# A linear-attention and rational-FFN kernel: the second batch's k'v products in one visit, its o's one slot each, casts of x by converting transfers

## The chip, the cores and the metric

The kernel runs on one core of one Trainium2 chip. A core has five engines that run their own instruction lists side by side and wait for each other by semaphores: TensorE (PE, matmuls), VectorE (DVE), ScalarE (ACT), GpSimd (POOL) and SyncE (SP, which here only issues transfers). The metric is the device time of one execution in microseconds (us); lower is better. Before the change it is 879.95 us, the median of 3 runs (879.93 to 879.99).

## The reference

Eight batches of 576 tokens, 8 heads of 64. Each head's attention is linear: k'v is one 64x64 matrix per head, o is q times it, and o is normalised per token and head. The 4608 tokens of 512 features then pass a feed-forward layer of 2048 hidden units whose activation is a rational function.

```python
kv  = einsum('bhsd,bhse->bhde', k, v)
out = einsum('bhsd,bhde->bhse', q, kv)
rms = sqrt(mean(out * out, axis=-1) + 1e-06)
x   = (out / rms * g_norm)          # heads side by side: [4608, 512]
h   = x @ w_in                      # [4608, 2048]
P   = a[0] + a[1]*h + a[2]*h**2 + a[3]*h**3
Q   = 1.0 + abs(b[0])*abs(h) + abs(b[1])*h**2
y   = (P / (Q + 1e-06)) @ w_out     # [4608, 512]
```

The two weights come as 64-bit words and are turned into fp32 on the chip.

## The kernel before

**Tiles and slots.** The tokens are cut into 9 tiles of 512: tile t (0 to 7) holds the first 512 tokens of batch t, and tile 8 the 64 tokens that each batch has left over. Each tile passes 16 slots, one for each chunk c of 128 hidden units. In slot (t, c) ACT and DVE turn h(t, c) into g(t, c) (`ew_a` to `ew_d`), PE makes the h of the next slot (`gemm1`, names h, lines L527 to L533), and adds the g of two slots before into the output's accumulators (`gemm2`, names acc, lines L590 to L601, LAG = 2). Beside this, the attention of the *next* tile is made, a step here and a step there, by the tables `attention` (tiles 1 and later) and `attention0` (tile 0). What each engine does is a list in program order: from `tc.manual_schedule()` on nothing is moved.

**Tile 0** is special. The weights are loaded, turned to fp32 (ACT: `signed` L206, `lowbits` L213; DVE: `conv_b1` L224, `conv_add` L228) and later split into a high and a low part while it runs; a table `schedule` says in which slot. Until the split is there the matmuls are plain fp32: a 128x512 matmul then stands as two records of 0.43 us in the trace. The split of x for tile 0 (`split_x0`) makes a high part by an ACT cast (L258), and a low part from it by a POOL negation (L250) and an accumulating transfer on POOL's queue (L251). It is first used by h(0, 8).

**The attention of tile 1, made during tile 0.** The four head pairs p go one after the other. `att_kv1` makes k'v of one pair (names kvp, 20 small matmuls, L351) in slots 1, 3, 5 and 7, and ACT copies it to kvf (L270). `att_o` makes o of that pair (names op, L430) in slots 2, 4, 6 and 8, and ACT squares and copies it (L438, L439). kvp and op share one PSUM buffer (`ps_at`, tag "at", one buffer), so each waits until ACT has read the one before. The transposed q of a pair, qr, has one buffer too: `fetch_q` for pair p + 1 is issued on SP right behind o of pair p (`fetch_next_q`), and waits for it. Means (ms, L451) and reciprocal roots stand in slot 9, the products of the leftover tokens (rest, L379) in slot 10. Tiles 2 and later make all four pairs of k'v in one visit (`att_kv4`).

**The front.** Before slot 0, batch 0's own attention is made in two halves of 256 tokens. Sums over a head (`first_ms`, L692) and the spreading of the reciprocal roots to all rows (`first_rb`, L708) work in NBLK blocks of BW tokens.

**SP's queue.** All loads go through SP, in program order: an entry that waits for a buffer holds up all behind it. A transfer also waits until the eighth one before it has landed.

Of the kernel before, what the change touches and what calls it, by code (L numbers as in the profile page):

```python
# [7 lines left out]
F32 = mybir.dt.float32  # L8
# [15 lines left out]
def linear_attention_then_rational_ffn(  # L24
# [38 lines left out]
    NC = 7  # L63
    HW = TW // 2
    MAIN = 8 * P
    NBLK = 4
    BW = HW // NBLK
    kv0 = [wpool.tile([P, 2, MAIN], F32, tag=g, name=f"first_{g}") for g in ("g4", "g5")]
    qa0 = wpool.tile([P, NPAIR * HW + NC], F32, tag="g6", name="first_qa")
# [100 lines left out]
        made[schedule["wi", c][1] + 1].append(("wi", c, None))  # L170

    EARLY = 8
    ON_VECTOR = (("wi", 6),)

    def unsplit(t, c):
        return t == 0
# [77 lines left out]
    def split_x0(g):  # L254
        pool, tag = ((xpool, "xA"), (wpool, "e"))[g]
        xt = pool.tile([P, 2, 2, TW], F32R, tag=tag, name=f"x_0_{g}")
        of = x0[:, 2 * g:2 * g + 2]
        ACT.copy(xt[:, :, 0], of)  # L258
        x.setdefault(0, []).extend((xt[:, p, 0], xt[:, p, 1]) for p in range(2))
        lows.append((xt[:, :, 1], xt[:, :, 0], of))  # L260

# [2 lines left out]
    def split_kv(t, pairs, ps):  # L266
        n = pairs.stop - pairs.start
        made = [ps[js, 0:n * D].rearrange("p (n d) -> p n d", n=n) for js in heads]
        for js, m in zip(heads, made):
            ACT.copy(kvf[js, pairs, js], m)  # L270
        if t == 1:
            return None
        for js, m in zip(heads, made):
            ACT.copy(kvh[js, pairs, js], m)

        def rest():
            for js in heads:
                DVE.tensor_tensor(kvl[js, pairs, js], kvf[js, pairs, js], f32(kvh[js, pairs, js]), ALU.subtract)
        return rest
# [28 lines left out]
    kvms, qrs, qs, sqs, rs, rbs, xf = {}, {}, {}, {}, {}, {}, {}  # L308

    def fetch_kv(t, p):  # L310
        tag, bufs = ("rb", 2) if p >= 2 and t > 1 else (f"kvm{p % 2}", 1)
        kvms[t, p] = work.tile([P, 2, 4, P], F32, tag=tag, name=f"kvm_{t}_{p}", bufs=bufs)
        nc.sync.dma_start(kvms[t, p], kv[t, p])

    def fetch_ends(t):
        kvms[t] = work.tile([P, 2, 3, P], F32, tag="kvt", name=f"kvt_{t}", bufs=1)
        nc.sync.dma_start(kvms[t], kv_rest[t])

    def fetch_q(t, p):
        qrs[t, p] = work.tile([P, TW], F32, tag="qr", name=f"qr_{t}_{p}", bufs=1)  # L320
        nc.sync.dma_start(qrs[t, p], qT[p, :, t * TW:(t + 1) * TW])

    def fetch_first_kv(t):
        if t < NB:
            for p in range(2):
                fetch_kv(t, p)
            fetch_ends(t)

    def fetch_last_kv(t, _):
        if t + 1 < NB:  # L330
            for p in range(2, NPAIR):
                fetch_kv(t + 1, p)
# [12 lines left out]
    def kv_products(t, ps, k, p):  # L345
        m = kvms.pop((t, p))
        ends = kvms[t][:, p // 2]
        for c in range(5):
            for js in heads:
                a, b = (m[:, 0, c], m[:, 1, c]) if c < 4 else (ends[:, 0], ends[:, 1 + p % 2])  # L350
                PE.matmul(ps[js, k * D:(k + 1) * D], a[:, js], b[:, js], start=(c == 0), stop=(c == 4))  # L351

    def att_kv1(t, p):
        ps = ps_at.tile([P, TW], F32, tag="at", name=f"kvp_{t}_{p}", bufs=1)
        kv_products(t, ps, 0, p)
        qs[t, p] = qrs.pop((t, p))
        split_kv(t, slice(p, p + 1), ps)

    def att_kv4(t, ps):
        if t >= NB:  # L360
            return None
        for p in range(NPAIR):
            kv_products(t, ps, p, p)
        fetch_first_kv(t + 1)
        return lambda: split_kv(t, slice(0, NPAIR), ps)

    def att_kv_of_third(t, _):
        return att_kv4(t, ps_at.tile([P, TW], F32, tag="at", name=f"kvp_{t}", bufs=1))() if t == 2 else None

    x_rest = dram.tile([NPAIR, P, NB * R], F32, tag="x_rest", name="x_rest", bufs=1)  # L370

# [50 lines left out]
    def att_o(t, p):  # L422
        if t == LAST:
            sqs[t, p] = work.tile([P, TW], F32, tag="at", name=f"sq_{t}_{p}", bufs=4)
            ACT.activation(sqs[t, p], xf[t, p], AF.Square)
            return
        ps = ps_at.tile([P, TW], F32, tag="at", name=f"op_{t}_{p}", bufs=1)
        q = qs.pop((t, p))
        if t == 1:
            PE.matmul(ps, kvf[:, p], q, start=True, stop=True)  # L430
        else:
            qh, ql = q
            PE.matmul(ps, kvh[:, p], ql, start=True, stop=False)  # L433
            PE.matmul(ps, kvl[:, p], qh, start=False, stop=False)  # L434
            PE.matmul(ps, kvh[:, p], qh, start=False, stop=True)  # L435
        sq = work.tile([P, TW], F32, tag="at", name=f"sq_{t}_{p}", bufs=4)
        xf[t, p] = xpool.tile([P, TW], F32, tag=f"xf{p}", name=f"xf_{t}_{p}")
        ACT.activation(sq, ps, AF.Square)  # L438
        ACT.copy(xf[t, p], ps)  # L439
        sqs[t, p] = sq  # L440
        if t == 1:
            if p + 1 < NPAIR:
                fetch_kv(t, p + 1)
            else:
                fetch_first_kv(t + 1)
            fetch_next_q(t, p)

    def att_ms(t, _):
# [41 lines left out]
    attention = {s: [] for s in range(NF)}  # L490
    for p in range(NPAIR):
        if p == 0:
            attention[0].append((att_kv_of_third, 0))
        attention[2 * p].append((att_q, p))
        attention[2 * p + 1].append((att_o, p))
        attention[(11, 12, 13, 13)[p]].append((att_norm, p))
    attention[3].append((fetch_last_kv, 0))
    attention[8] += [(att_rest, 0), (att_ms, 0)]
    attention[9].append((att_rstd, 0))
    fillat = {att_norm: 1, att_kv_of_third: 1, att_rest: 1, att_q: 1, att_rstd: 2}  # L500
    attention[10] += [(att_rd, 0), (att_rb, 0), (att_rb, 1)]

    fillat0 = {}
    attention0 = {s: [] for s in range(NF)}
    for f, at in ((att_kv1, [1, 3, 5, 7]), (att_o, [2, 4, 6, 8]), (att_ms, [9]), (att_rstd, [9]), (att_rd, [10]), (att_rest_first, [10]), (fetch_last_kv, [11]), (att_rb, [11, 11]), (att_norm, [12, 12, 13, 13])):
        for p, k in enumerate(at):
            attention0[k].append((f, p))

# [224 lines left out]
            DVE.tensor_copy(x0[:, p, halves[0]], o0[p][0])  # L733
    for u in at_slot(0, -1)[:1]:
        fetch_w(u)
    fetch_kv(1, 0)
    fetch_ends(1)
    fetch_q(1, 0)
    for u in at_slot(0, -1)[1:]:
        fetch_w(u)  # L740
    ms0 = ps_at.tile([P, TW], F32, tag="ms", name="ms_0", bufs=1)
    first_ms(0)
    for p in range(NPAIR):
# [40 lines left out]
    for i, (t, c) in enumerate(slots[:-1]):  # L784
        q_made = ew_a(t, c, ph)
        for todo in lows:

            tc.add_manual_dep(low_by_transfer(*todo).ins, q_made.ins.name, beside, reason="negated beside h")
        lows.clear()
        if i:  # L790
            ew_d(*slots[i - 1])
        rest = {0: [], 1: [], 2: []}
        shifts = []
        convs = [lambda u=(k, n), j=j: conv_add(u, both if j is None else (one, two)[j]) for k, n, j in made.get(i, [])]

        ew_b(t, c, ph, convs[:1])
        if i == LAG:
            ph = gemm1(0, i + 1)
        if i >= LAG:
            gemm2(*slots[i - LAG])  # L800
            if slots[i - LAG][1] == NF - 1:
                evacuate(slots[i - LAG][0])
        for u in at_slot(2, i):
            split_w(u)
        if i in (1, 3):
            split_x0(i // 3)
        if i == 0:
            ph = h0[1]
        elif i in (1, 3):
            ph = gemm1(0, i + 1)  # L810
        if t + 1 < NTILE:
            for step, p in (attention0 if t == 0 else attention)[c]:
                todo_dve = step(t + 1, p)
                if todo_dve:
                    rest[fillat0.get(step, 2) if t == 0 else fillat[step]].append(todo_dve)
            for u in at_slot(0, i):
                fetch_w(u)
        for u in at_slot(1, i):
            signed(u)
            lowbits(u, both, "V" if u in ON_VECTOR else "S")  # L820
            shifts.append(u)
        rest[2] += convs[1:]
        if t == 0 and c == NF - 3:
            rest[2] += [split(1, p) for p in range(NPAIR // 2)]
        if t and c == NF - 2:
            ph = h_last
        elif 4 <= i < len(slots) - 2:
            ph = gemm1(*slots[i + 1])
            if 0 < t < NTILE - 1 and c == NF - 3:
                h_last = gemm1(t, NF - 1)  # L830
        if c == NF - 2 and t < NTILE - 1:
            xl = [split(t + 1, p) for p in range(NPAIR // 2 if t == 0 else 0, NPAIR)]
            if t == 0:
                rest[0] += xl
            for k in range(2 if t else 0):
                rest[k].append(xl[k])
                rest[2].append(xl[2 + k])
        if i == 0:
            rest[2].append(lambda: conv_add(u2, one))
        rest[2] += [lambda u=u: conv_b1(u, both) for u in shifts]  # L840
        ew_c(t, c, lambda k: [f() for f in rest[k]])
# [55 lines left out]
```

## Time and profile before

| | |
|---|---|
| median of the runs | 879.95 us |
| the profiled execution's own time | 879.79 us |
| its span, first to last instruction | 877.7 us |
| granted TensorE clock | 0.999 |
| PE busy | 870.7 us, 99% |
| DVE busy | 757.7 us, 86% |
| ACT busy | 687.5 us, 78% |
| POOL busy | 73.3 us, 8% |
| SP's transfers | 65.81 MB |
| POOL's transfers | 9.44 MB |

In the rows that follow, times are us from the start of the span. A row of the chain of waits is "start, duration, what": the chain is followed back from the last instruction, at each step to what released it. A row of the timeline is "start, duration, engine line operation, out<-in, count", with the idle time before it and its releaser in brackets; PEld is PE's loading of weights, which runs ahead of the matmul, and SPq is SP's queue. The ends of matmuls are modelled, so a busy PE is read from the chain and from PEld's gaps, not from its busy share.

### The profile page before, as it was taken

Reading aid. Unit: us, or ns where it says so; the run is one execution under the profiler, and the core shown is the slowest. Engines: PE = TensorE matmul, PEld = TensorE weight load, DVE = VectorE, ACT = ScalarE, POOL = GpSimd, SP = SyncE. Lnnn points to the kernel's source line nnn. Section 1 sums busy time; section 2 is a strip of 40 time slices with the busy share of each in tenths; the row PEclk is TensorE's granted clock in tenths of the full one; section 3 lists DMA queues with packets and bytes.
Section 4 is the critical chain, followed back from the end, with each engine's and each line's share of the span. In section 5 each row is a group of like instructions: output and inputs, shape, how many; then the busy total and the mean of one; then the engine's idle time right before and its main releaser. Section 6 shows DMA issues by size and latency. Waiting matters only on the chain.

```text
span 877.7 us, 11994 instructions
## 1 busy us (share of the span) xinstructions
PE 870.7 (99%) x4468; PEld 683.9 (78%) x4468; DVE 757.7 (86%) x1185; ACT 687.5 (78%) x1142; POOL 73.3 (8%) x63
## 2 busy tenths in 40 slices
PE   9999999999999999999999999999999999999997
PEld 7545657888888888878888888888878887888886
DVE  4988998979987998879887998799879987998887
ACT  5999889877876788777877787768867786787665
POOL 2131435413000000000000000000000000000000
PEclk9999999999999999999999999999999999999999
DMA  9987638554122203040303111020102020201001
GB/s 364 406 262 226 145 73 216 138 127 97 60 73 90 50 6 115 30 122 1 119 19 104 31 61 72 25 50 17 69 12 50 13 84 1 49 1 49 1 0 49
DMA packets 32650, 76.27 MB, mean 87 GB/s; under 512 B 6032, under 2 KB 7568, under 8 KB 32592
## 3 DMA queue, kind: packets, MB, share of 16 engines
q1 hardware_dynamic: 29600, 65.81, 22.0%
q0 software_dynamic: 2848, 9.44, 5.9%
q8 instruction: 35, 0.57, 0.3%
q10 hardware_dynamic: 144, 0.26, 0.1%
q14 instruction: 23, 0.19, 0.1%
HBM read 55.45 MB, written 10.62 MB: 75 GB/s over the span
## 4 chain that ended last, share of the span: by engine, by line
PE 91%; DVE 5%; ACT 2%; issue 1%; DMA 1%; SPq 0%; ACTq 0%
PE h L531 14%; PE h L532 13%; PE h L533 13%; PE acc L599 12%; PE acc L601 12%; PE acc L600 12%; PE acc L590 5%; PE h L527 2%; PE kvp L351 2%; PE ms L451 1%; DMA first_g<-in_first_dram 1%; PE op L435 1%; PE op L433 1%; PE op L434 1%; DVE u L545 1%
## 5 line engine op out<-in xcount | busy, mean ns | idle before, releaser
L541 ACT ACTIVATE d<-h 128x512 f32<-128x512 f32 x143 | 85.6, 599 | 139.4 <-PE h L533 138.3
L543 DVE SCALAR_TENSOR_TENSOR q<-d,b1abs,q 128x512 f32<-128x512 f32 x143 | 107.2, 749 | 83.7 <-ACT q L542 83.5
L531 PE MATMUL h<-x,wihl 128*128 128x512 f32 (+1 forms) x420 | 166.2, 396 | 0.0
L532 PE MATMUL h<-x,wihl 128*128 128x512 f32 (+1 forms) x420 | 162.7, 387 | 0.0
L533 PE MATMUL h<-x,wihl 128*128 128x512 f32 (+1 forms) x420 | 162.6, 387 | 0.0
L599 PE MATMUL acc<-woh,gl 128*128 128x512 f32 x316 | 123.1, 389 | 0.1
L600 PE MATMUL acc<-wol,gh 128*128 128x512 f32 x316 | 122.9, 389 | 0.0
L601 PE MATMUL acc<-woh,gh 128*128 128x512 f32 x316 | 122.9, 389 | 0.0
L554 ACT ACTIVATE d<-q,bias 128x512 f32<-128x512 f32 x143 | 105.6, 738 | 13.9 <-DVE q L543 12.5
L544 ACT ACTIVATE u<-h,na 128x512 f32<-128x512 f32 x143 | 112.5, 787 | 0.0
L555 ACT ACTIVATE d<-d,bias 128x512 f32<-128x512 f32 x143 | 103.6, 725 | 4.7
L561 DVE SCALAR_TENSOR_TENSOR u<-u,na,d 128x512 f32<-128x512 f32 x143 | 106.7, 746 | 0.0
L551 DVE SCALAR_TENSOR_TENSOR u<-u,na,h 128x512 f32<-128x512 f32 x143 | 106.1, 742 | 0.6
L559 DVE SCALAR_TENSOR_TENSOR q<-q,d 128x512 f32<-128x512 f32 x143 | 98.4, 688 | 0.2 <-ACT d L555 0.2
L545 DVE TENSOR_TENSOR u<-u,h 128x512 f32<-128x512 f32 x143 | 98.0, 685 | 0.0
L542 ACT ACTIVATE q<-h,abg 128x512 f32<-128x512 f32 x143 | 97.9, 685 | 0.0
L531 PEld LDWEIGHTS h<-x,wihl 128*128 128x128 f32 x420 | 78.9, 188 | 24.0 <-issue 6.2
L532 PEld LDWEIGHTS h<-x,wihl 128*128 128x128 f32 x420 | 78.9, 188 | 17.0 <-issue 1.2
L533 PEld LDWEIGHTS h<-x,wihl 128*128 128x128 f32 x420 | 78.9, 188 | 16.2
L578 DVE TENSOR_TENSOR gl<-u,gh 128x512 fp32r<-128x512 f32 x127 | 90.8, 715 | 0.0
L567 DVE SCALAR_TENSOR_TENSOR u<-q,u 128x512 f32<-128x512 f32 x127 | 87.5, 689 | 2.5
L577 ACT CAST gh<-u 128x512 fp32r<-128x512 f32 x127 | 80.3, 632 | 3.5 <-DVE u L567 3.4
(170 smaller groups left out, 1403.0 us busy)
## 6 DMA issues: line engine op xcount, KB each, us to landing
kvm<-in_kv_dram SPq DMA_DIRECT2D x28, 512.0 KB
raw_wo<-in_w_out_dram SPq DMA_DIRECT2D x8, 1024.0 KB
out_dram<-ob SPq DMA_DIRECT2D x16, 512.0 KB
qr<-in_qT_dram SPq DMA_DIRECT2D x28, 256.0 KB
rb<-rd SPq DMA_DIRECT2D x28, 256.0 KB
raw_wi<-in_w_in_dram SPq DMA_DIRECT2D x6, 1024.0 KB
wihl<-wiw POOLq DMA_DIRECT2D x6, 512.0 KB, 4.7
kvt<-in_kv_rest_dram SPq DMA_DIRECT2D x7, 384.0 KB
```

The source lines that it names most:

```text
L531: PE.matmul(ph, wh, xl, start=(kc == 0), stop=False)
L532: PE.matmul(ph, wl, xh, start=False, stop=False)
L533: PE.matmul(ph, wh, xh, start=False, stop=(kc == NPAIR - 1))
L543: q_made = DVE.scalar_tensor_tensor(q, d, b1abs, q, ALU.mult, ALU.add)
L544: ACT.activation(u, ph, AF.Identity, bias=na[:, 2:3], scale=na[:, 3:4])
L545: DVE.tensor_tensor(u, u, ph, ALU.mult)
L551: DVE.scalar_tensor_tensor(u, u, na[:, 1:2], ph, ALU.add, ALU.mult)
L554: ACT.activation(d, q, AF.Ln, bias=bias[:, 2:3], scale=QSC)
L561: DVE.scalar_tensor_tensor(u, u, na[:, 0:1], d, ALU.add, ALU.mult)
L599: PE.matmul(o, gl[:, ss], wh, start=(c == 0), stop=False)
L600: PE.matmul(o, gh[:, ss], wl, start=False, stop=False)
L601: PE.matmul(o, gh[:, ss], wh, start=False, stop=(c == NF - 1))
```

## The change

- `att_kv1` is gone. All four pairs' k'v of the second batch are made by `att_kv4` in slot 3 of tile 0, and copied by two ACT copies of 64x4x64 instead of eight of 64x64. The o's stand in slots 4, 5, 6 and 7, and the leftover products in slot 9, ahead of the means.
- The loads follow: all of batch 1's k and v (kvm, kvt) are fetched in the front, behind the weights that are fetched there; batch 2's first two pairs of k and v are fetched by `att_kv4`, so in slot 3; qr of pairs 1 to 3 is still fetched behind the o before it.
- NBLK goes from 4 to 2: blocks of 128 tokens.
- The two high parts of tile 0's x are made by converting transfers on POOL's queue, issued in slot 0; the low parts follow one slot after the other.
- The low bits of the fourth pair of weight chunks (wi6) move from DVE to ACT.

```diff
-    NBLK = 4
+    NBLK = 2
-    ON_VECTOR = (("wi", 6),)
+    ON_VECTOR = ()
 def split_x0(g):
-        ACT.copy(xt[:, :, 0], of)
+        POOL.dma_start(xt[:, :, 0], of)
-        lows.append((xt[:, :, 1], xt[:, :, 0], of))
+        return xt[:, :, 1], xt[:, :, 0], of
 def fetch_kv(t, p):
-        tag, bufs = ("rb", 2) if p >= 2 and t > 1 else (f"kvm{p % 2}", 1)
+        tag, bufs = ("rb", 2) if p >= 2 else (f"kvm{p % 2}", 1)
-    def att_kv1(t, p): ...
-    def att_kv_of_third(t, _):
-        return att_kv4(t, ps_at.tile(...))() if t == 2 else None
+    def att_kv(t, _):
+        if t <= 2:
+            return att_kv4(t, ps_at.tile(...))()
 def att_o(t, p):
-            if p + 1 < NPAIR:
-                fetch_kv(t, p + 1)
-            else:
-                fetch_first_kv(t + 1)
             fetch_next_q(t, p)
-    for f, at in ((att_kv1, [1, 3, 5, 7]), (att_o, [2, 4, 6, 8]), (att_ms, [9]), (att_rstd, [9]), (att_rd, [10]), (att_rest_first, [10]), ...
+    for f, at in ((att_kv, [3]), (att_o, [4, 5, 6, 7]), (att_rest_first, [9]), (att_ms, [9]), (att_rstd, [9]), (att_rd, [10]), ...
 (front)
-    fetch_kv(1, 0)
-    fetch_ends(1)
-    fetch_q(1, 0)
     for u in at_slot(0, -1)[1:]:
         fetch_w(u)
+    fetch_first_kv(1)
+    fetch_last_kv(0, 0)
+    fetch_q(1, 0)
 (slots)
-        if i in (1, 3):
-            split_x0(i // 3)
+        if i == 0:
+            x0_lows = [split_x0(g) for g in range(2)]
+        if i in (1, 2):
+            lows.append(x0_lows[i // 2])
```

PE around slots 3 to 5 of tile 0, before: kvp_1_1 is k'v of the second batch's pair 1, op_1_1 its o, kvm and kvt are k and v, acc with g_0_2 is the output's part of chunk 2.

```order
L527 MATMUL h_0_4_522<-x0_144,wiw4_405 128x512 x4
L351 MATMUL kvp_1_1_527<-kvm_1_1_487 64x64 x8
L351 MATMUL kvp_1_1_527<-kvt_1_238 64x64 x2
L590 MATMUL acc_0_0_473<-wow2_452,g_0_2_499 128x512
L590 MATMUL acc_0_1_474<-wow2_452,g_0_2_499 128x512
L590 MATMUL acc_0_2_475<-wow2_452,g_0_2_499 128x512
L590 MATMUL acc_0_3_476<-wow2_452,g_0_2_499 128x512
L430 MATMUL op_1_1_571<-qr_1_1_489,kvf_128 128x512
L527 MATMUL h_0_5_585<-x0_144,wiw4_405 128x512 x4
```

The same place on PE now:

```order
L518 MATMUL h_0_4_475<-x0_144,wiw4_383 128x512 x4
L351 MATMUL kvp_1_480<-kvm_1_0_242 64x64 x8
L351 MATMUL kvp_1_480<-kvt_1_246 64x64 x2
L351 MATMUL kvp_1_480<-kvm_1_1_244 64x64 x8
L351 MATMUL kvp_1_480<-kvt_1_246 64x64 x2
L351 MATMUL kvp_1_480<-kvm_1_2_248 64x64 x8
L351 MATMUL kvp_1_480<-kvt_1_246 64x64 x2
L351 MATMUL kvp_1_480<-kvm_1_3_250 64x64 x8
L351 MATMUL kvp_1_480<-kvt_1_246 64x64 x2
```

All four pairs stand in one run behind h(0, 4); acc with g_0_2 and op_1_0 follow, and op_1_1 stands one slot, h(0, 5) and acc with g_0_3, behind op_1_0.

SP's queue before, from the load of the chunk pair wo6 to the q of pair 2 of the second batch (qr_1_2; raw_ are weights):

```order
L191 DMA raw_wo6_439<-in_w_out_dram 128x2x512
L313 DMA kvm_1_1_487<-in_kv_dram 128x1024
L321 DMA qr_1_1_489<-in_qT_dram 128x512
L191 DMA raw_wi12_491<-in_w_in_dram 128x2x512
L191 DMA raw_wo8_493<-in_w_out_dram 128x2x512
L191 DMA raw_wi14_540<-in_w_in_dram 128x2x512
L313 DMA kvm_1_2_577<-in_kv_dram 128x1024
L321 DMA qr_1_2_579<-in_qT_dram 128x512
```

And now, from wo6 to wo10:

```order
L191 DMA raw_wo6_402<-in_w_out_dram 128x2x512
L191 DMA raw_wi12_444<-in_w_in_dram 128x2x512
L191 DMA raw_wo8_446<-in_w_out_dram 128x2x512
L313 DMA kvm_2_0_521<-in_kv_dram 128x1024
L313 DMA kvm_2_1_523<-in_kv_dram 128x1024
L317 DMA kvt_2_525<-in_kv_rest_dram 128x768
L191 DMA raw_wi14_529<-in_w_in_dram 128x2x512
L321 DMA qr_1_1_564<-in_qT_dram 128x512
L191 DMA raw_wo10_566<-in_w_out_dram 128x2x512
```

The q of pair 1 went from before wi12 to behind wi14, and three loads of the third batch's k and v stand ahead of it.

More of the change, by code (lines that the diff above doesn't have):

```diff
@@ L351, in kv_products @@
                 PE.matmul(ps[js, k * D:(k + 1) * D], a[:, js], b[:, js], start=(c == 0), stop=(c == 4))
[L353 to L357, printed above, removed]
     def att_kv4(t, ps):
@@ L365, in att_kv4 @@
         return lambda: split_kv(t, slice(0, NPAIR), ps)
-    def att_kv_of_third(t, _):
-        return att_kv4(t, ps_at.tile([P, TW], F32, tag="at", name=f"kvp_{t}", bufs=1))() if t == 2 else None
+    def att_kv(t, _):
+        if t <= 2:
+            return att_kv4(t, ps_at.tile([P, TW], F32, tag="at", name=f"kvp_{t}", bufs=1))()
     x_rest = dram.tile([NPAIR, P, NB * R], F32, tag="x_rest", name="x_rest", bufs=1)
@@ L427, in att_o @@
         ps = ps_at.tile([P, TW], F32, tag="at", name=f"op_{t}_{p}", bufs=1)
-        q = qs.pop((t, p))
+        q = qrs.pop((t, p)) if t == 1 else qs.pop((t, p))
         if t == 1:
@@ L492, in linear_attention_then_rational_ffn @@
         if p == 0:
-            attention[0].append((att_kv_of_third, 0))
+            attention[0].append((att_kv, 0))
         attention[2 * p].append((att_q, p))
@@ L499, in linear_attention_then_rational_ffn @@
     attention[9].append((att_rstd, 0))
-    fillat = {att_norm: 1, att_kv_of_third: 1, att_rest: 1, att_q: 1, att_rstd: 2}
+    fillat = {att_norm: 1, att_kv: 1, att_rest: 1, att_q: 1, att_rstd: 2}
     attention[10] += [(att_rd, 0), (att_rb, 0), (att_rb, 1)]
@@ L504, in linear_attention_then_rational_ffn @@
     attention0 = {s: [] for s in range(NF)}
-    for f, at in ((att_kv1, [1, 3, 5, 7]), (att_o, [2, 4, 6, 8]), (att_ms, [9]), (att_rstd, [9]), (att_rd, [10]), (att_rest_first, [10]), (fetch_last_kv, [11]), (att_rb, [11, 11]), (att_norm, [12, 12, 13, 13])):
+    for f, at in ((att_kv, [3]), (att_o, [4, 5, 6, 7]), (att_rest_first, [9]), (att_ms, [9]), (att_rstd, [9]), (att_rd, [10]), (fetch_last_kv, [11]), (att_rb, [11, 11]), (att_norm, [12, 12, 13, 13])):
         for p, k in enumerate(at):
```

## Prediction

> **What bounds the kernel now.** I read first the chain of waits of the page, then the chain in order of time around tile 0, since the change touches only tile 0 and what stands before it.
>
> ```profile
> PE 91%; DVE 5%; ACT 2%; issue 1%; DMA 1%; SPq 0%; ACTq 0%
> ```
>
> So time is won or lost where PE waits or works less. In order of time, tile 0:
>
> ```profile
> 48.87 1.13 PE op L430 x2
> 49.99 3.43 PE h L527 x8
> 53.43 3.43 PE acc L590 x8
> 56.86 0.73 PE kvp L351 x20
> 57.59 3.63 PE h L527 x8
> ...
> 64.65 0.86 PE op L430 x2
> ...
> 72.38 0.73 PE kvp L351 x20
> 73.11 0.43 PE h L531
> 73.54 0.23 PE h L532
> ...
> 86.55 1.00 PE ms L451 x8
> 87.55 0.43 PE h L531
> ...
> 93.92 1.08 PE rest L379 x32
> 95.01 0.43 PE h L531
> ...
> 132.22 2.48 PE kvp L351 x80
> 134.71 0.43 PE h L531
> ```
>
> From 48.87 on the chain is PE alone, with nothing between its pieces. Before that it runs over ACT and DVE, but PE's weight loads show how little that is worth; they stand idle over the usual gap only here:
>
> ```profile
> 48.87 0.30 PEld L430 LDWEIGHTS op<-qr,kvf 128*128 128x128 f32 x2 [0.94 <-ACT kvf L270]
> 49.40 0.19 PEld L527 LDWEIGHTS h<-x,wiw 128*128 128x128 f32 x1 [0.24 <-DVE u L561]
> ```
>
> A steady weight load has 0.24 idle ahead of it (the second row), so this one came 0.70 late. A load stands one matmul, 0.43, ahead of its own matmul when PE is full, and about 0.1 ahead when PE is empty: PE stood for 0.70 - 0.43 + 0.10 = 0.37 us. From h(0, 0) to here PE is otherwise full, so relieving ACT and DVE can win that and no more.
>
> **Second, the DMA engines.** They bound nothing yet, but have no room either:
>
> ```profile
> 4.00:46.00 42.00, 41.02 (x352) 25.96 (x352) 31.93 (x60) 32.36 (x59) 7.55 (x11) 1.00 1.03 408
> 46.00:48.00 2.00, 2.00 (x6) 0.95 (x5) 1.97 (x5) 1.90 (x3) 0.00 (x0) 1.00 1.09 259
> 48.00:50.00 2.00, 1.89 (x5) 0.66 (x4) 1.97 (x5) 1.97 (x5) 0.00 (x0) 1.00 1.10 324
> 50.00:56.00 6.00, 6.00 (x15) 2.65 (x15) 5.42 (x9) 5.79 (x10) 2.76 (x1) 1.00 1.03 407
> ```
>
> The last two columns are the DMA engines' share and GB/s: full from 4 to 56 us at about 408 GB/s, with a dip at 46 to 50. The dip is the accumulating transfer of x's first half, issued at 42.82 and long in landing:
>
> ```profile
> 42.82 1.39 POOL L251 DMA_DIRECT2D x<-x  x1 [0.32 <-POOL x L250]
> ...
> 56.23 1.24 POOL L251 DMA_DIRECT2D x<-x  x1 [0.31 <-POOL x L250]
> DMA to landing us min/median/max: 5.5/7.9/10.3
> ```
>
> It moves 0.52 MB, and the dip lost (408 - 259) x 2 + (408 - 324) x 2 = 0.47 MB more: it costs 0.99 MB of full traffic, 2.4 us. SP's queue at that time:
>
> ```profile
> 44.81 0.37 SPq L191 DMA_DIRECT2D raw_wi<-in_w_in_dram  x1
> 45.23 1.17 SPq L313 DMA_DIRECT2D kvm<-in_kv_dram  x1
> 50.02 0.34 SPq L321 DMA_DIRECT2D qr<-in_qT_dram  x1
> 50.47 0.38 SPq L191 DMA_DIRECT2D raw_wo<-in_w_out_dram  x1
> 50.90 0.46 SPq L313 DMA_DIRECT2D kvm<-in_kv_dram  x1
> SPq L321 <- DMA qr<-in_qT_dram: 4.2, 1, 4.2
> ```
>
> The last row is of SP's waits from 50.9 to 66: the q of pair 3 waits 4.2 us for the q of pair 2 to land, so from 50.90 + 0.46 = 51.36 to 55.56. A quarter of a megabyte issued at 50.02 took 5.54 us, because wi14 and a kvm (1.57 MB) were issued just ahead and the engines were full. It was not late: its o is at 64.65, 14.6 us after the issue.
>
> **The change part by part.**
>
> *k'v in one visit (win).* A visit of 20 costs 0.73 and slows what follows by 0.20 (3.63 against 3.43 at 57.59; L531 0.43 against 0.23 for its neighbours): 4 x 0.93 = 3.72. The visit of 80 at 132.22 costs 2.48 + 0.20 = 2.68. Win 1.04 us, all on PE's path.
>
> *Casts of x off ACT, fewer copies of kvf (win, small).* A cast stands ahead of the copy that PE waited for at 48.87; with it gone that wait goes: 0.37. The other cast and the six copies saved lie beside PE. What is late next: acc of chunk 1.
>
> ```profile
> L258 ACT CAST x<-x 128x1024 fp32r<-128x1024 f32 x2 | 2.1, 1033 | 0.0
> L213 ACT ACTIVATE raw_wi<-raw_wi 128x1024 int32<-128x1024 uint32 (+1 forms) x6 | 6.4, 1071 | 0.0
> ...
> 37.36 3.60 PE L590 MATMUL acc<-wow,g 128*128 128x512 f32 x8
> ...
> 33.46 0.69 DVE L211 TENSOR_SCALAR raw_wi<-raw_wi 128x1024 int32<-128x1024 uint32 x1
> ...
> 35.44 0.69 DVE L567 SCALAR_TENSOR_TENSOR g<-q,u 128x512 f32<-128x512 f32 x1
> ```
>
> It began at 37.36; without a visit (0.93) and an o (0.86) ahead of it PE comes there at 35.6, and g(0, 1) ended at 35.44 + 0.69 = 36.1.
>
> *Low bits of wi6 on ACT.* The DVE row at 33.46 goes, which brings g(0, 1) 0.6 forward, to 35.5. I charge 0.14 for the weight load that still comes late. ACT takes 1.07 for the low bits, in the slot in which it loses a cast of 1.03 and two copies: no charge.
>
> *rest beside ms (win).* Each slows the matmul behind it by 0.20 (0.43 against 0.23); together only once: 0.20.
>
> *Blocks of 128.* Half as many ms and spreading matmuls, twice as wide; reciprocal roots on ACT and DVE over 128 columns instead of 64. No row has the new shapes. At best half of the two stretches goes:
>
> ```profile
> 12.15 0.92 PE ms L692 x28
> 13.16 0.32 ACT r L283
> 19.01 1.05 PE op L708 x32
> ```
>
> that is 1.0 us; at worst nothing is won and the three ACT operations of the first round take half of 0.32 more each, 0.5. I take 0, since both stand on the same short path. With a stall later on, as below, what is won or lost before it changes only the stall's length, and the ends fall away.
>
> *o's a slot each.* PE's work is the same. But each o's q has one buffer, and is fetched behind the o before: from issue to need there was 14.6 us, and now there is one h and one acc, 6.86 us.
>
> *Loads.* Ahead of pair 1's q SP's queue now holds, against what stood ahead of and with pair 2's q above: kvm of pair 3 and two of the third batch (3 x 512 KB by the shapes in the order above, four bytes an element), a kvt (384 KB), less one qr (256 KB): 1664 KB or 1.70 MB more. At 408 GB/s 4.2 us. POOL's queue adds the second accumulating transfer, now a slot earlier (issued about 49, before 56.23): 2.4 us; and the two casts, 0.52 MB each. No row shows a converting transfer without accumulating; its bounds are 1.3 us (its bytes at 408 GB/s) and 2.4 (the accumulating one, the nearest row: same queue, same size, but it also reads what it adds to). I take the middle, 3.7 for two.
>
> So pair 1's q lands at 55.56 + 4.2 + 2.4 + 3.7 = 65.9 us, as long as the engines stay full; with SP's eight transfers ahead they do. The loads of k and v for slot 3 and of the weights come by the same sum 1 to 10 us before their use.
>
> *When PE wants it.* acc of chunk 3 ended at 56.86. Up to there PE now makes 2.68 + 0.86 + 0.14 instead of 2 x 0.93 + 2 x 0.86 + 0.37: 56.6. So PE stands from 56.6 to 65.9: **9.3 us lost at the second o**. Behind op_1_1 in PE's list is all of the rest, and ACT waits for it in slot 5 too. The later q's are not late: ahead of pair 2's only wo10 and an accumulating transfer are left, about 5.4 us after 65.9, where PE needs 7.7.
>
> *Sum.* -1.04 - 0.37 - 0.20 + 0.14 = -1.47 without the stall; +9.3 with it: +7.8. Against the profiled execution's own 879.79 (span 877.7): 887.6. The median of the runs shown is 0.16 higher, so 887.8.
>
> Whether order holds on SP's queue decides between the two sums. The row for it is pair 2's q: 5.54 us for 256 KB, where it and the 1.57 MB ahead of it take 4.5 us at 408 GB/s, and alone it would take 0.6. That is a queue worked off in order, and 887.8. The Trainium skill, page "DMA: Bandwidth & Descriptors", section "Queues, rings and completion order", says that completion is "not FIFO per issuing engine". By that sentence a small load could land ahead of larger ones, and the sum would be 878.5; the trace's one case does not agree, and I give it the chance of rival 1.
>
> **The rivals.**
>
> *1. The q passes the loads ahead of it: not slower.* If it lands within 7 us of its issue at about 49.8, by 56.6, there is no stall, and the sum is 879.95 - 1.47 = 878.5. For this it must pass all but 2.8 MB of what the engines have still to move, some 6.5 MB by the same count. Against it: pair 2's q did not pass 1.57 MB.
>
> *2. ACT was the path.* The chain before 48.87 goes over ACT and DVE; if that is what PE follows, the casts (2 x 1.03) and one wide copy less would win 2 us more with no stall: about 876.5. Against it: weight loads without a gap.
>
> *3. A second stall at the third o.* Its slack is 2.3 us; if wo10 and the accumulating transfer take longer than counted, up to 3 us more: 891.
>
> *4. Cheap traffic.* If the casts cost their bytes alone and the accumulating one is not ahead, the q lands at 62.4: 884.3. That is the lower end of my own case; casts that cost as much as accumulating ones give 67.0 and 888.9, the upper end.
>
> **How the numbers follow.** The stall as forecast, with its ends: 0.79. Rival 3: 0.05. A shorter stall than any of these ends, 880 to 883: 0.04. Rival 1: 0.10. Rival 2: 0.02. The likeliest gives 887.8. The range must leave out no more than 2 in 10: from 882.5 to 891 it leaves out rivals 1 and 2 and part of the short stalls. About 0.2% (1.8 us) is what a measurement of this kernel can tell from no change: 878.2 to 881.7. Rival 1 lies at 878.5, so 0.06 of it counts as the same and 0.04 as faster; with rival 2 faster has 0.06, with the shortest stalls the same has 0.08, and slower 0.86.
>
> **What would show it.** In the chain after: one kvp of 80 near 43 us and 2.7 long with its tail; no wait of op for kvf; a PE gap of 5 to 11 us ahead of the second op, ended by a DMA of qr, near 56 to 66; ms right behind rest; DMA at its full share to some 66 us. Wrong would make me a q that lands soon after 50, or full engines that end by 56, since then everything else is a win of 1 to 2 us.

## Result and profile after

The changed kernel takes 889.22 us (median of 4 runs, 888.05 to 889.48), the kernel before, on the same chip, 879.94 us (879.78 to 879.99). The ratio is 1.0103, 95% interval 1.0086 to 1.0121: slower by 9.3 us, where the prediction said 7.8. The profiled execution took 889.10 us, with a span of 887.3 us at a mean granted clock of 0.993 (before: 879.79, 877.7 and 0.999).

The chain of waits in order of time, from the start of tile 0 (the rows of before began at 48.87 with the first o):

```profile
20.38 12.29 PE h L518 x40
32.67 6.99 PE acc L581 x16
39.66 3.43 PE h L518 x8
43.09 2.48 PE kvp L351 x80
45.57 3.63 PE acc L581 x8
49.20 0.87 PE op L425 x2
50.08 0.02 issue
50.09 14.93 DMA qr<-in_qT_dram
65.02 0.14 issue
65.16 2.05 PE op L425 x2
67.20 4.87 PE h L518 x8
...
96.43 1.08 PE rest L374 x32
97.51 1.00 PE ms L442 x8
```

Up to the first o it is PE alone, as predicted: one visit of 80, no wait for kvf. Then the chain leaves PE for the q of pair 1, which is issued at 50.09 and lands at 65.02. The second o follows it, and then come two things that the prediction did not have: the second o takes 2.05 us instead of 0.87, and the h behind it 4.87 instead of 3.43.

How long PE really stood is in the timeline's row of the second o (the brackets hold the idle time before it and what ended it):

```profile
65.16 2.05 PE L425 MATMUL op<-qr,kvf 128*128 128x512 f32 x2 [8.23 <-DMA qr<-in_qT_dram]
```

Why the matmuls behind it are slow is in the windows (the last three columns are the granted clock, the DMA engines' share and GB/s):

```profile
26.00:34.00 8.00, 8.00 (x20) 3.61 (x19) 7.89 (x14) 7.28 (x10) 0.00 (x0) 1.00 1.10 394
...
46.00:58.00 12.00, 10.93 (x26) 4.56 (x24) 10.79 (x16) 11.72 (x17) 3.98 (x2) 1.00 1.07 322
...
62.00:64.00 2.00, 0.00 (x0) 0.00 (x0) 1.89 (x4) 0.00 (x0) 1.42 (x2) 0.50 1.04 416
...
66.00:68.00 2.00, 2.00 (x4) 0.82 (x3) 0.00 (x0) 0.76 (x2) 0.00 (x0) 0.50 0.95 201
...
70.00:72.00 2.00, 2.00 (x6) 0.85 (x5) 0.07 (x1) 0.38 (x1) 0.00 (x0) 1.00 0.04 11
```

The clock falls to half while PE stands, and it is still at half when PE starts again: full only from 70 us on. The DMA engines are full until the q lands, and nearly empty from 70 us on (11 GB/s): the q is kept by transfers that are wanted later than it.

### The profile page after: what moved, and what is told of

The parts are those of the page before. It is cut to its first block, busy times and chain, and to the rows that moved or that the text cites. A ratio compares the mean times of both kernels' runs of the same rounds, so it can differ in the third digit from the quotient of the medians.

```text
span 887.3 us, 11865 instructions
## 1 busy us (share of the span) xinstructions
PE 871.7 (98%) x4404; PEld 683.9 (77%) x4404; DVE 757.7 (85%) x1184; ACT 686.3 (77%) x1135; POOL 74.6 (8%) x65
## 4 chain that ended last, share of the span: by engine, by line
PE 92%; DVE 3%; DMA 2%; ACT 1%; issue 0%; SPq 0%; ACTq 0%
PE h L522 13%; PE h L523 13%; PE h L524 13%; PE acc L590 12%; PE acc L591 12%; PE acc L592 12%; PE acc L581 6%; PE h L518 3%; PE kvp L351 2%; DMA qr<-in_qT_dram 2%; PE ms L442 1%; DMA first_g<-in_first_dram 1%; PE op L430 1%; PE op L429 1%; PE op L428 1%; PE op L425 1%
```

## The experiments

**1. Whose order? The q on a queue of its own.**

```diff
-        nc.sync.dma_start(qrs[t, p], qT[p, :, t * TW:(t + 1) * TW])
+        (ACT if t == 1 and p else nc.sync).dma_start(qrs[t, p], qT[p, :, t * TW:(t + 1) * TW])
```

> The changed kernel, but the q's of pairs 1 to 3 of the second batch are issued on ACT's own queue instead of SP's; same bytes, same buffer. Theory A (the q of pair 1 waits because SP's queue is worked off in order and 4.8 MB stand ahead of it): on a queue of its own it lands about 2.5 us after its issue. The issue stands behind ACT's copy of the first o, which ended at 55.7, so it lands near 58.2, where PE wants it at 56.8: a stall of 1 to 2 us, no drop of TensorE's clock, 880.3 us (879.3 to 881.5). Theory B (the DMA engines are full, whatever the queue, and every transfer of that time lands some 15 us after its issue): the q lands at 65 or later, 889 us or more.

Measured: 883.87 us (883.72 to 884.74), ratio 1.0047 [1.0032, 1.0062]. Its chain:

```profile
53.03 7.08 DMA qr<-in_qT_dram
...
60.25 2.05 PE op L425 x2
62.30 5.44 PE h L518 x8
```

The wait from issue to landing is halved, 14.93 to 7.08 us, but 256 KB on an otherwise empty queue still take 7 us. Order on SP's queue is about half of the wait; the other half stays when the queue is another. The time lies between the two expectations.

**2. The third batch's k and v fetched behind the last o.**

```diff
-        fetch_first_kv(t + 1)
+        if t > 1:
+            fetch_first_kv(t + 1)
...
+                if p + 1 == NPAIR:
+                    fetch_first_kv(t + 1)
```

> The changed kernel, but the third batch's first k and v (1.44 MB) are fetched behind the second batch's last o, as before, and not in slot 3. Theory A: 1.44 MB less stand ahead of the q of pair 1, at 408 GB/s 3.5 us: it lands at 61.5 instead of 65.0. PE then stands 4.8 us, which is still longer than the 3.0 us after which the clock fell, so the slow stretch stays: 885.7 us (884.8 to 886.5). If the place in the queue did not matter: 889.

Measured: 885.26 us (884.65 to 886.18), 1.0062 [1.0047, 1.0077].

```profile
50.04 11.13 DMA qr<-in_qT_dram
61.31 2.05 PE op L426 x2
```

The q lands at 61.17, 3.85 us sooner, for 1.44 MB less ahead of it (3.5 us at 408 GB/s). What stands ahead on the queue is paid by about its bytes, as the prediction's sum has it; landing and time lie within 0.5 us of the expectation.

**3. The casts on ACT as before, alone.**

```diff
-        POOL.dma_start(xt[:, :, 0], of)
+        ACT.copy(xt[:, :, 0], of)
...
-        if i == 0:
-            x0_lows = [split_x0(g) for g in range(2)]
-        if i in (1, 2):
-            lows.append(x0_lows[i // 2])
+        if i in (1, 3):
+            split_x0(i // 3)
```

> The changed kernel with the high parts of x cast by ACT in slots 1 and 3 as before, so without the two converting transfers, and with the second accumulating transfer a slot later (issued about 56 instead of 49). Theory A: two converting transfers cost 2.9 us of the engines' time by the dips of the changed kernel's trace, and 1.0 to 2.5 us of the accumulating one move behind the q: it lands at 59.6 to 61.1, 884.0 to 885.5 us with the clock's drop. If converting transfers cost next to nothing: 887.5 or more.

Measured: 881.28 us (881.15 to 883.16), 1.0023 [1.0013, 1.0033]: 2.7 us below the lower end of the expectation. Chain, and POOL's issues of the accumulating transfers:

```profile
49.13 0.78 issue
49.91 1.11 PE op L425 x2
51.04 8.51 DMA qr<-in_qT_dram
59.68 1.10 PE op L425 x2
60.78 3.43 PE h L518 x8
```

```profile
43.53 1.39 POOL L251 DMA_DIRECT2D x<-x  x1 [0.32 <-POOL x L250]
...
57.23 1.24 POOL L251 DMA_DIRECT2D x<-x  x1 [0.31 <-POOL x L250]
```

The q lands at 59.55, 5.5 us sooner, at the early end of the expectation (59.6). With the casts back in slots 1 and 3 the second accumulating transfer goes back too, from 49.04 to 57.23, and all of it stands behind the q. Casts 2.9 and that transfer 2.6, both estimates from the dips (worked out below), make the 5.5. What the expectation had wrong is the clock: it counted its drop, but with a stall of 1.80 us the clock stays at full in the profiled run, and op and h have nearly their usual lengths. The price is a wait of 0.78 at the first o. Three of its nine runs took 883.0 to 883.2. None of these has a profile, but their mean granted clock is 0.997, the lowest of the nine (the others 0.998 to 1.0), so it likely fell in them.

**4. The stall kept, PE kept busy in it.** Nine matmuls whose result nobody uses stand ahead of the second o.

```diff
+        if (t, p) == (1, 1):
+            busy = ps_at.tile([P, TW], F32, tag="ms", name="busy", bufs=1)
+            for _ in range(9):
+                PE.matmul(busy, x0[:, 0, 0:P], x0[:, 1], start=True, stop=True)
```

> The changed kernel with nine idle 128x512 fp32 matmuls into a free PSUM buffer ahead of the second o: 7.7 us of work in the 8.4 us in which PE stands and waits for q. Theory C (the half clock from 59.8 to 69.8 us comes from PE standing idle, and costs the 1.2 us of the o and 1.4 us of the h that ran at it): the clock stays at 1.00, the stall's end stays at 65, 886.6 us (886.0 to 887.2). If the clock falls for another reason, or the slow stretch is contention for memory: 889.2.

Measured: 886.87 us (886.69 to 887.25), 1.0081 [1.0064, 1.0097].

```profile
49.96 15.02 DMA qr<-in_qT_dram
...
65.11 1.10 PE op L429 x2
```

The q lands as late as before, but the clock stays at 1.00 and o takes 1.10. The engines move as much as before (418 GB/s from 62 to 64 us, 416 in the changed kernel), so it isn't contention. The half clock is caused by PE's idling, and is worth 889.22 - 886.87 = 2.4 us, a quarter of the whole loss.

**5. The stall taken away.** The q's of pairs 1 and 2 get buffers that tile 0 doesn't use, and are fetched in the front.

```diff
-        qrs[t, p] = work.tile([P, TW], F32, tag="qr", name=f"qr_{t}_{p}", bufs=1)
+        tag = ("qr", "qh", "ql", "qr")[p] if t == 1 else "qr"
+        qrs[t, p] = work.tile([P, TW], F32, tag=tag, name=f"qr_{t}_{p}", bufs=1)
...
-        if t == 1:
-            fetch_next_q(t, p)
+        if t == 1 and p in (0, 3):
+            fetch_next_q(t, p or 2)
...
-    fetch_q(1, 0)
+    for p in range(3):
+        fetch_q(1, p)
```

> The changed kernel, but the q of pairs 1 and 2 get buffers of their own (qh and ql, which are not used before tile 2) and are fetched in the front behind pair 0's; only pair 3's is fetched later, behind the first o. If the late q explains the whole loss (8.4 us of stall and 2.6 us of half clock after it), no DMA stands in the chain at the second o, the granted clock stays at 1.00, and the rest of the change is left: 879.94 - 1.04 - 0.37 - 0.20 + 0.13 + 0.3 (h(0, 0) starts 0.3 later with blocks of 128) = 878.8. If the two casts by transfer or the second k'v load slow something else as well (the weights, k and v of slot 3), it stays above 880, and the chain names another transfer.

Measured: 878.22 us (878.02 to 878.33), ratio 0.9981 [0.9972, 0.9989]: faster than the kernel before. The expectation had 878.8.

```profile
49.03 0.86 PE op L426 x2
49.89 3.43 PE h L519 x8
53.32 3.43 PE acc L582 x8
56.75 0.86 PE op L426 x2
```

```profile
46.00:58.00 12.00, 12.00 (x30) 5.31 (x29) 10.59 (x16) 11.71 (x18) 3.80 (x2) 1.00 1.07 321
```

Behind the first load there is no DMA in the chain any more, and PE is busy throughout this stretch, though the engines are as full from 46 to 58 as in the changed kernel (321 GB/s against 322) with the same dips. So the late q, with what the clock adds, is the whole loss: the two spans differ by 887.3 - 876.3 = 11.0 us. Of these, 8.2 are the idle time, (2.05 - 0.87) + (4.87 - 3.43) = 2.6 the half clock, and 0.2 that h(0, 0) began that much earlier here.

**6. The same with blocks of 64 in the front** (NBLK = 4), and **7.** the changed kernel with only that, and **8.** the kernel before with only blocks of 128.

```diff
-    NBLK = 2
+    NBLK = 4
```

> As the one before, but with the front's blocks of 64 tokens back (NBLK = 4). If blocks of 128 lengthen the front by 0.3 us, as h(0, 0) at 20.38 instead of 20.06 says, nothing hides it here: 0.3 us less than the one before, about 878.5. If the later start came from other parts of the change (the order of loads), no difference.

> The changed kernel with nothing else than blocks of 64 tokens in the front (NBLK = 4). The prediction's sentence: what is won or lost ahead of the stall changes only the stall's length. Then h(0, 0) starts at about 20.1, PE reaches the second o 0.3 us sooner and waits 0.3 us longer: 889.2, unchanged, q lands at 65.0 as before. The rival, that the q lands sooner by as much (the engines are not the bound): 888.9.

> The kernel before with nothing else than blocks of 128 tokens in the front (NBLK = 2). No stall follows there, so what the front loses is lost: 879.94 + 0.3 = 880.25. The prediction's ends for it were -1.0 and +0.5, its value 0.

Measured: 6: 878.09 us (877.84 to 878.44), 0.9980 [0.9971, 0.9988]. 7: 888.54 (888.20 to 889.25), 1.0099 [1.0086, 1.0113]. 8: 880.08 (879.91 to 880.23) beside 879.89, 1.0002 [0.9993, 1.0011].

The expected 0.3 isn't there: 0.1 (number 6 against 5) to 0.2 (number 8), too little to tell from nothing. I had taken it from h(0, 0) beginning at 20.38 instead of 20.06. Most of that is the first load (first_g), which the block size can't touch: it lands at 8.90 in the kernel before, at 9.06 in number 8 and at 9.12 in the changed kernel. From landing to h(0, 0): 20.06 - 8.90 = 11.16 before, 20.31 - 9.06 = 11.25 in number 8, so 0.09 for blocks of 128; in the changed kernel 20.38 - 9.12 = 11.26. The prediction's 0 was right to within 0.2. In number 7 the q lands at 65.00, where it was 65.02, though PE comes to the second o 0.2 sooner. Its time is a little below the changed kernel's because the clock came back earlier there (h 3.97 us instead of 4.87).

**9. Low bits on DVE again**, in the version of number 6.

```diff
-    ON_VECTOR = ()
+    ON_VECTOR = (("wi", 6),)
```

> The version with early q and blocks of 64 tokens (878.09), but the low bits of wi6 are made by DVE again, as in the kernel before. The prediction charged 0.14 for g(0, 1) with these bits on ACT and gave DVE's row 0.6 us ahead of g(0, 1). If that holds, PE waits 0.6 longer at acc of chunk 1: 878.7. If DVE has room there, no difference: 878.1.

Measured: 878.67 us (878.44 to 878.94), 0.58 above number 6. The weight load of acc of chunk 1, in number 6 and then here:

```profile
35.72 0.30 PEld L582 LDWEIGHTS acc<-wow,g 128*128 128x128 f32 x2 [0.67 <-DVE g L559]
```

```profile
36.37 0.30 PEld L582 LDWEIGHTS acc<-wow,g 128*128 128x128 f32 x2 [1.29 <-DVE g L559]
```

It stands 0.62 longer, as priced. With these bits left on DVE, 0.58 us of what the rest of the change wins would be lost again.

**10. Casts on ACT**, in the version of number 6 (the edit of number 3).

> The version with early q and blocks of 64 tokens (878.09), but the casts of x's high parts are on ACT again, as in the kernel before. It prices what the converting transfers win at the first o. The prediction's term is 0.37 (the wait for kvf in the kernel before): 878.5. The rival comes from the changed kernel with casts on ACT: there the first o ended at 51.02 instead of 50.08, so with k'v in one visit the cast costs the first o about 1.0: 879.1.

Measured: 878.93 us (878.83 to 879.24), 0.84 above number 6.

```profile
48.83 0.75 issue
49.58 1.10 PE op L426 x2
```

That is 0.75 of waiting and 1.10 instead of 0.86 for the first o, 0.99 together; 0.14 of it doesn't show in the time, since PE came to the first o at 48.83 here and at 48.97 in number 6. The cast stands ahead of the copies of kvf on ACT. With k'v in one visit right ahead of the o it costs 0.84 by the medians, not the 0.37 of the kernel before: the rival's price, or near it. So the converting transfers win 0.84 where they don't delay a q. In the changed kernel they, and the second accumulating transfer that moves with them, cost far more: number 3 is 7.9 us faster.

**11. The q on ACT's queue and the casts on ACT** (edits of numbers 1 and 3): what is the 7.08 us of number 1?

> The changed kernel with the q of pairs 1 to 3 on ACT's queue and the casts of x on ACT, so that the second accumulating transfer is issued at about 57 instead of 49 and POOL's queue holds nothing when q is issued at about 53 to 54. On ACT's queue alone the q took 7.08 us with POOL's accumulating transfer under way. If it shared the engines with that transfer and SP's loads, it now takes 4 us or less, lands at about 57.5, and the second o waits 0 to 1 us: 879 to 880. If SP's loads alone hold it up, it takes 7 us still and lands at 60 to 61: about 882.

Measured: 884.27 us (884.13 to 884.37), 1.0050 [1.0035, 1.0065].

```profile
54.88 6.01 DMA qr<-in_qT_dram
...
61.03 2.05 PE op L425 x2
63.08 3.89 PE h L518 x8
```

The DMA queues in this run, as packets, MB and share of the 16 engines (q1 is SP's queue, q10 ACT's): from 54.8 to 58.2 us, from 58.2 to 60.6, and, for the q of pair 3, issued at 71.30 when SP's queue is empty, from 72.2 to 73.8:

```profile
q1 hardware_dynamic: 374, 1.43, 102.5%
...
q1 hardware_dynamic: 141, 0.52, 54.2%
q10 hardware_dynamic: 144, 0.26, 28.9%
...
q10 hardware_dynamic: 144, 0.26, 49.3%
```

The expectation that POOL's transfer shared the time falls: the second accumulating transfer is issued only at 57.20, and from 54 to 60 the engines move 414 GB/s, without a dip such as these transfers make (322 above). Still the q took 6.01 us. So SP's loads alone hold up a q on another queue for most of the 7.08. The q lands at 60.89, as the second expectation has it; the time is 2 us above that expectation's since it had no half clock (o 2.05 and h 3.89, 1.65 us together) and the q came at the late end of its 60 to 61.

The Trainium skill, page "DMA: Bandwidth & Descriptors", section "Queues, rings and completion order", says that a transfer's semaphore increment lands only after every earlier write of that DMA engine, across its queues. That could keep a q waiting whose bytes have long arrived, but it isn't what the rows show. The q's first packet comes only at 58.2, 3.3 us after the issue; its 0.26 MB then take 2.4 us beside SP's loads, and the landing follows 0.3 us behind the last packet. With SP's queue empty the first packet comes 0.9 us after the issue and all have passed 1.6 us later. So full engines cost the q 2.4 us before its first byte and 0.8 us by sharing. What holds the first byte back isn't settled.

## Why the prediction came out right, point by point

**The verdict and the mechanism** held: q of pair 1 lands late, PE stands at the second o, and without that the change is a gain (number 5). Rivals 1, 2 and 3 fell: the q waits for the bytes ahead of it on SP's queue (number 2), ACT was not worth 2 us (number 5 wins 1.7 in all), and no DMA stands in the chain at the third o. Rival 4's cheap traffic is part right, see below.

**k'v in one visit, -1.04; rest beside ms, -0.20; wait for kvf, -0.37; chunk 1, +0.14.** The visit has its 2.48 and one slow follower of 3.63. rest and ms stand back to back. The weight load of chunk 1 came 0.45 late (0.69 of idle time ahead of it against the usual 0.24), and 16 matmuls of acc took 6.99 instead of 2 x 3.43 = 6.86: 0.13. The sum without a stall, -1.47, can be held against number 5. Its span is 1.4 shorter than the one before, with a start of h(0, 0) 0.16 later: -1.6 from there on. By the medians it is 878.22 - 879.94 = -1.7.

**The q's landing, 65.9; measured 65.02.** Issue and the bytes on SP's queue were right (number 2). The mis-sized term is the casts: 3.7 taken, the middle between 1.3 and 2.4 each. From 26 to 34 the engines moved 394 GB/s where the kernel before moved 410, 0.13 MB less; with the casts' own 1.05 MB that is 1.18 MB, 2.9 us for two at 408 GB/s. So casts are near the cheap end, hardly more than their bytes. Two accumulating transfers cost (408 - 322) x 12 = 1.03 MB and their own 1.05, 5.1 us together, 2.6 each (taken: 2.4). 55.56 + 4.2 + 2.6 + 2.9 = 65.3. The two prices are estimates from dips; together they are borne out by number 3, which has neither the casts nor the second accumulating transfer ahead of the q: it lands at 59.55 there, and 55.56 + 4.2 is 59.8.

**The stall, 9.3; measured 8.2.** The q came 0.9 sooner than forecast and the front's late start brought PE 0.3 later.

**What the sum lacked: the clock, +2.6.** No term stood for what PE does after it has idled. In the trace of before PE never stands long enough in tile 0 to show it, but a forecast of 9.3 us of idling should have raised the question. There was a hint in the kernel: while it waits for its first loads, PE runs matmuls on zeros whose result nobody uses, by a function called `warm`. The two errors, a stall 1.1 us too long and a clock left out, have opposite signs; that the forecast missed by only 1.4 us of 9.3 is in part luck.

**The ledger by the spans:** -1.56 (the wins), +0.32 (start), +8.23 (stall), +2.62 (clock) = +9.6; measured 887.3 - 877.7 = +9.6. The runs' +9.3 is 0.3 less since the time outside the span was 1.8 us here and 2.1 before.

## What to carry to other kernels

When steps that each fetch their input behind the step before are pushed closer together, count the bytes between issue and need on every queue, not the size of the transfer: 256 KB took 15 us here. A small load that paces PE belongs early, into a buffer that is free at that time; that turned +9.3 us into -1.7 (number 5; with blocks of 64, number 6, the lowest median of this study, -1.8). And price a stall with what follows it: a few us of idle PE cost half the clock for several us more.

## What the runs showed of the hardware

**The half clock comes in steps of 3.41 us.** The granted clock is 1.00 or 0.50; a mean over a slice of 0.2 us tells the edge in it. The slices with the fall and the return, in the changed kernel, then in numbers 1 and 11:

```profile
59.60:59.80 0.20, 0.00 (x0) 0.00 (x0) 0.20 (x1) 0.19 (x1) 0.06 (x1) 0.80 1.01 410
69.80:70.00 0.20, 0.20 (x1) 0.10 (x1) 0.20 (x1) 0.20 (x1) 0.00 (x0) 0.60 0.13 51
```

```profile
59.20:59.40 0.20, 0.00 (x0) 0.00 (x0) 0.20 (x1) 0.20 (x1) 0.00 (x0) 0.92 1.15 456
66.00:66.20 0.20, 0.20 (x1) 0.00 (x0) 0.00 (x0) 0.00 (x0) 0.00 (x0) 0.51 1.15 461
```

```profile
60.40:60.60 0.20, 0.00 (x0) 0.00 (x0) 0.00 (x1) 0.20 (x2) 0.00 (x0) 0.62 1.21 266
63.80:64.00 0.20, 0.20 (x2) 0.19 (x1) 0.20 (x2) 0.20 (x1) 0.20 (x1) 0.85 0.17 31
```

From 59.72 to 69.96, 59.37 to 66.20 and 60.45 to 63.86; read in the same way, 61.31 to 68.13 in number 7 and 60.35 to 67.18 in number 2: 10.24, 6.83, 3.41, 6.82 and 6.83 us, so three, two, one, two and two times 3.41. The Trainium skill, page "TensorE: Matmul & The Clock Gate", section "Part 1: The HAM clock gate", gives a window of 3413 ns that runs freely, and these lengths agree with it. It puts the fall behind at least one idle window of about 3.4 us. Here the clock fell 2.8 us (changed kernel: 65.16 - 8.23 = 56.93 to 59.72), 2.5 us (number 1), 3.5 us (number 2), 4.6 us (number 7) and 2.6 us (number 11) after PE went idle. The ends of matmuls are modelled, but even from the start of the last matmul, 0.59 us before its end, it is 3.1 and 3.2 us in numbers 1 and 11; so an idle time below that figure is no safe one. In number 3's profiled run PE idled 1.8 us and kept its clock.

What the half clock costs doesn't follow from the length of the idling: 3.42 us of it cost 3.2 us in number 1 (5.44 - 3.43 and 2.05 - 0.86), 8.39 us of it 1.7 us in number 7. That it depends on where the window happens to stand fits these rows and the spread of 1.4 us among the changed kernel's runs, against 0.2 of the kernel before (the fastest run of the changed kernel, 888.05 us, has the highest granted clock of its four, 0.995); no run moved the window to show it.

**A converting transfer costs hardly more than its bytes, an accumulating one twice as much**: by the dips 1.45 us against 2.6 us of full traffic for 0.52 MB. The queues' own rows in the changed kernel say the same. They give packets, MB and share of the 16 engines, from 26 to 34 us, when POOL's queue (q0) has the two casts, and from 46 to 58, when it has the two accumulating transfers:

```profile
q1 hardware_dynamic: 566, 2.11, 70.4%
q0 software_dynamic: 514, 1.02, 38.5%
...
q1 hardware_dynamic: 753, 2.87, 62.0%
q0 software_dynamic: 501, 0.99, 44.5%
```

A MB of the casts takes 38.5 / 1.02 = 37.7% of the engines' time in its stretch where a MB of SP's loads takes 33.4%, 1.1 times as much; a MB of the accumulating transfers takes 44.9% against 21.6%, 2.1 times as much.
